# Sliding-window attention with a SwiGLU layer on one core: blocks 12 and 13 transposed by DMA, block 10 transposed three parts earlier, and another cut of the last output tile

## The chip, the cores and the metric

The kernel runs on one core of one Trainium2 chip. The metric is the device time of the kernel in microseconds (us). Before the change the median of three runs is 249.16 us (249.16 to 249.19). The profiled execution of the same kernel spans 248.5 us from its first to its last instruction, at a granted TensorE clock of 1.000.

## What is computed

Two stages, one behind the other. First attention with a sliding window of 128 keys and four "sink" keys that every query sees, for 4 batches, 8 heads, 768 positions and a head size of 64. Its output, laid out as 3072 tokens of 512 values, goes through an RMS norm and a gated layer:

```python
scores = scale * np.matmul(q, k.transpose(0, 1, 3, 2))
keep = is_sink | in_window          # in_window: 0 <= query - key < 128
a = softmax(np.where(keep, scores, -1e9));  x = a @ v
xn = x / np.sqrt(np.mean(x * x, axis=-1, keepdims=True) + 1e-06) * rms_g
g = xn @ w_gate
out = (g / (1 + exp(-g)) * (xn @ w_val)) @ w_out    # 512 -> 1536 -> 512
```

## The kernel before

**Blocks and groups.** The 3072 tokens are 24 blocks of 128 (`g` = 0 to 23; six to a batch, `b, t = divmod(g, 6)`). Four blocks make a group of 512 tokens (`G` = 0 to 5), which is what the gated layer works on. For a block, GpSimd issues the loads of q, k and v (`unit_load`; they become bf16 on the way), q and k are transposed so that the head dimension lies on the partitions (`unit_t`, into the tile `qkT` of the batch), TensorE makes the scores (`unit_s`, tile `pT`), ScalarE their exponentials (`et`), and TensorE multiplies by v (`unit_attend`, tile `pv`). VectorE divides by the sums (`rden`, `x`), ScalarE sums the squares (`sq`), VectorE makes the RMS scale and the scaled block (`xr`), and the block is transposed once more into `xnt` of its group (`unit_x`).

**Parts.** The gated layer of a group is a list of parts. A pair of parts for each slice of the hidden dimension is `gate` (tile `pg`, then tanh on ScalarE into `th`) and `val` (tile `pvl`, then two VectorE operations that give `p` and `hT`). They are followed by three parts for each output tile of 128 tokens (`parts_o`): 12 matmuls into `po`, a halving copy by ScalarE into `osb` (three buffers), and a store that SyncE issues. Group 0 comes as two halves of 256 tokens, `fa` and `fb`; the list of `fb` with the output tiles has 24 parts, 0 to 23. The later groups have 24 parts of `gate` and `val` and then 12 of output.

**Order.** `run(parts, slots)` walks the list of parts and ahead of part `s` calls the units whose slot number is `s` or lower, in the order of their numbers, and what is left after the last part. So attention for later blocks is woven by hand into the gated layer of an earlier group. For `fb` the slots are written out in `FIRST`; for later groups `step(g, p)` makes them, with `AT` giving each block its part. In group 1 the blocks 9 to 13 start at parts 0, 8, 14, 20 and 28. In these lists TensorE, SyncE and GpSimd keep the order as written (`MANUAL`), while the order of VectorE and ScalarE is set by the framework's planner, which takes an instruction when it reckons that its inputs are ready and takes the one written first when several are. In `fa` VectorE keeps the written order too.

**Transposes of q and k.** There are two ways. On TensorE: eight 128 x 128 transposes (L245) into one PSUM bank `pqk`, and a ScalarE copy of 128 x 1024 out of it (L279). By DMA: SyncE issues two transposing DMAs (L271), for q and for k, and TensorE and ScalarE do nothing. `by_dma(g)` says which; before, blocks from 14 on that don't start a batch go by DMA. `step` gives a TensorE transpose to the step two blocks earlier and a DMA transpose to the step three blocks earlier, four parts into it: block 12 comes at part 12 of group 1 and block 13 at part 18. Block 10 stands in `FIRST` at 21. Blocks 12, 13 and so on write `qkT` of their batch; two such tiles exist, and batch 2 takes the one that batch 0 had.

**PSUM.** One pool of eight banks serves all of TensorE's outputs; a matmul can wait for a bank that ScalarE or VectorE has yet to empty.

**The last tile.** `parts_last` cuts the last output tile into two halves of 256 columns. The first is copied by ScalarE and stored by SyncE. The second is copied in two pieces of 128 columns, by ScalarE (L698) and VectorE (L693), out of the same bank, and stored by two DMAs, from ScalarE's queue and from SyncE's.

**Semaphores of the DMAs.** The framework gives the DMAs of SyncE and ScalarE eight semaphores ("lanes") in turn, in the order in which they are issued. A DMA that takes a lane waits until the lane's previous DMA has landed. When the program ends (L904), SyncE waits for the lanes one after another, from the first to the eighth.

Of the kernel before, what the change touches and what calls it, by code (L numbers as in the profile page):

```python
# [9 lines left out]
ALU = mybir.AluOpType  # L10
ACT = mybir.ActivationFunctionType
FP32 = mybir.dt.float32
# [3 lines left out]
P = 128  # L16
# [12 lines left out]
def kernel(  # L29
# [13 lines left out]
    nc = tc.nc  # L43

    B, H, S, D = q.shape
    DM = H * D
# [4 lines left out]
    NT = S // P  # L51
    NB = B * NT
    HP = H // 2
    KTN = DM // P
    FTN = DFF // P
# [7 lines left out]
    NEG = -32768.0  # L63
    RMS_EPS = 1e-6 * RSQRT_SCALE ** 2
    MS_SCALE = RSQRT_SCALE / math.sqrt(DM)
    DMA_T_FROM = 14
    DMA_X_FROM = 12
    LD = 15
    FA = FTN
# [15 lines left out]
    opool = ctx.enter_context(tc.tile_pool(name="opool", bufs=3))  # L85
# [8 lines left out]
    wo = const.tile([P, FTN, DM], BF16, name="wo")  # L94
# [98 lines left out]
    with tc.manual_schedule(engines={mybir.EngineType.Pool, mybir.EngineType.DVE}):  # L193
        load_q(1)
        nc.gpsimd.affine_select(
            out=ident, in_=ident, compare_op=ALU.not_equal, fill=1.0,
# [3 lines left out]
            out=amasks[:, 1, 0, :], in_=amasks[:, 1, 0, :], compare_op=ALU.is_ge,  # L200
# [3 lines left out]
            out=amasks[:, 1, 1, :], in0=amasks[:, 1, 0, :], scalar1=-1.0, scalar2=NEG,  # L204
            op0=ALU.mult, op1=ALU.add,
# [17 lines left out]
            out=sel[:, P:P + NS], in_=sel[:, P:P + NS], compare_op=ALU.not_equal,  # L223
# [19 lines left out]
    def transposes(ps, src, c0):  # L243
        for hp in range(HP):
            nc.tensor.transpose(  # L245
                out=ps[:, c0 + hp * P:c0 + (hp + 1) * P],
                in_=src[:, 2 * hp:2 * hp + 2, :], identity=ident,
            )
# [11 lines left out]
        )  # L260

    def by_dma(g):
        return g >= DMA_T_FROM and g % NT > 0

    def unit_t(g):
        b, t = divmod(g, NT)
        if t == 0:
            QKT[b] = qkt.tile([P, 2, HP, S], BF16, name="qkT")
        if by_dma(g):
            for i, src in enumerate((QS.pop(g), KS_.pop(g))):  # L270
                nc.sync.dma_start_transpose(  # L271
                    out=QKT[b][:, i, :, t * P:(t + 1) * P],
                    in_=src.rearrange("p h d -> p (h d)"),
                )
            return
        ps = psum.tile([P, 512], FP32, name="pqk", tag="b1").bitcast(BF16)
        transposes(ps, QS.pop(g), 0)
        transposes(ps, KS_.pop(g), HP * P)
        nc.scalar.copy(  # L279
            out=QKT[b].rearrange("p i h s -> p (i h) s")[:, :, t * P:(t + 1) * P],  # L280
            in_=ps.rearrange("p (x c) -> p x c", c=P),
        )

    def unit_sink(b):
        ks = sink.tile([P, HP * KSW], BF16, name="ksk")
        nc.vector.memset(ks, 0.0)
        ksv = ks.rearrange("p (h c) -> p h c", c=KSW)
        for hi in range(2):
            pr = slice(hi * D, (hi + 1) * D)
            nc.scalar.copy(  # L290
                out=ksv[pr, :, hi * NS:(hi + 1) * NS],
                in_=QKT[b][pr, 1, :, 0:NS],
            )
        KSK[b] = ks
        vs = sink.tile([P, H, VW], BF16, name="vsk")
        for half in range(2):
            ps = psum.tile([P, 512], FP32, name="pvs", tag="b1")
            hs = slice(half * 4, half * 4 + 4)
            for i in range(4):
                h = half * 4 + i  # L300
                at = P - (32 * (h // 2) + NS * (h % 2))
                nc.tensor.matmul(
                    out=ps[:, i * VW:(i + 1) * VW], lhsT=sel[:, at:at + P],
                    rhs=V16[b][:, 0, h, :], start=True, stop=True,
                    skip_group_check=True,
                )
            nc.scalar.copy(
                out=vs[:, hs, :], in_=ps[:, 0:HW].rearrange("p (h c) -> p h c", c=VW),
            )
        VSK[b] = vs  # L310

    def unit_sink_scores(b, t):

        w = 2 * P
        ps = psum.tile([P, 512], FP32, name="pss", tag="b1")
        for hp in range(HP):
            nc.tensor.matmul(
                out=ps[32 * hp:32 * hp + KSW, 0:w],
                lhsT=KSK[b][:, hp * KSW:(hp + 1) * KSW],
                rhs=QKT[b][:, 0, hp, t * P:(t + 2) * P],  # L320
                start=True, stop=True,
            )
# [165 lines left out]
    def unit_attend(g):  # L488

        if g % NT >= 2:  # L490
            unit_sink_av(g)
        for u in range(2):
            unit_av(g, u)
# [139 lines left out]
    HT = {}  # L633
# [43 lines left out]

    def parts_last(G, tb):

        def half(c):  # L680
            po = psum.tile([P, 512], FP32, name="po", tag="b1")
            n = DM // 2
            for ft in range(FTN):
                nc.tensor.matmul(  # L684
                    out=po[:, 0:n], lhsT=HT[(G, ft // 2)][:, ft % 2, tb * P:(tb + 1) * P],
                    rhs=wo[:, ft, c * n:(c + 1) * n], start=(ft == 0), stop=(ft == FTN - 1),
                )
            row = (G * GB + tb) * P
            for i in range(1 + c):
                m = n // (1 + c)  # L690
                osb = opool.tile([P, m], FP32, name=f"ol{c}{i}", bufs=1)
                if i:
                    nc.vector.tensor_scalar(  # L693
                        out=osb, in0=po[:, i * m:(i + 1) * m], scalar1=0.5, scalar2=None,
                        op0=ALU.mult,
                    )
                else:
                    nc.scalar.mul(osb, po[:, 0:m], 0.5)  # L698
                (nc.sync, nc.scalar)[c - i].dma_start(
                    out=out[row:row + P, c * n + i * m:c * n + (i + 1) * m], in_=osb,  # L700
                )

        return [lambda: half(0), lambda: half(1)]

    def parts_o(G, tb):
        st = {}

        def part(i):
            if i == 0:
                st["po"] = psum.tile([P, 512], FP32, name="po", tag="b1")  # L710
            for ft in range(4 * i, 4 * i + 4):
                nc.tensor.matmul(  # L712
                    out=st["po"], lhsT=HT[(G, ft // 2)][:, ft % 2, tb * P:(tb + 1) * P],
                    rhs=wo[:, ft, :], start=(ft == 0), stop=(ft == FTN - 1),
                )
            if 4 * i + 4 == FTN:
                osb = opool.tile([P, DM], FP32, name="osb")

                nc.scalar.mul(osb, st["po"], 0.5)  # L719
                row = (G * GB + tb) * P  # L720
                nc.sync.dma_start(out=out[row:row + P, :], in_=osb)

        return [lambda i=i: part(i) for i in range(FTN // 4)]


    def step(g, p):

        b, t = divmod(g, NT)
        slots = [[] for _ in range(7)]
        if g < NB:  # L730
            if t in (2, 4):
                slots[0].append(lambda: unit_sink_scores(b, t))
            slots[0].append(lambda: unit_s(g))
            if t == 1:
                slots[2].append(lambda: unit_sink(b))
        if g <= NB:
            slots[0].append(lambda: unit_attend(g - 1))
        if g + 2 < NB and not by_dma(g + 2):
            slots[4].append(lambda: unit_t(g + 2))
        if g + 3 < NB and by_dma(g + 3):  # L740
            slots[4].append(lambda: unit_t(g + 3))
        for n in LOADS.pop(0) if LOADS else ():
            slots[1].append(lambda n=n: unit_load(n))
        return [(p + i, u) for i, us in enumerate(slots) for u in us]
# [14 lines left out]
    with tc.manual_schedule(engines=MANUAL_ALL):  # L759
# [35 lines left out]
            out=masks, in0=amasks, scalar1=-1.0 / NEG, scalar2=1.0,  # L795
            op0=ALU.mult, op1=ALU.add,
# [23 lines left out]
        (19, lambda: unit_x(5)),  # L820
        (19, lambda: unit_t(9)),
        (20, lambda: unit_attend(7)),
        (21, lambda: unit_t(10)),
        (22, lambda: unit_sink_scores(1, 2)),
        (22, lambda: unit_s(8)),
        (23, lambda: unit_x(6)),
# [27 lines left out]
    with tc.manual_schedule(engines=MANUAL):  # L854
# [54 lines left out]
```

The softmax here doesn't subtract the row's maximum and nothing guards it: scores larger than these inputs give would overflow.

## Time and profile before

| What | Value |
|---|---|
| Time, median of 3 | 249.16 us |
| Span of the profiled execution | 248.5 us |
| TensorE busy | 241.8 us, 97% |
| VectorE busy | 163.6 us, 66% |
| ScalarE busy | 145.2 us, 58% |
| GpSimd busy | 105.1 us, 42% |
| Group 1 (`pg` of group 1 to `pg` of group 2) | about 68.2 to 107.9 us: TensorE 39.70 of 39.70, ScalarE 28.43, VectorE 27.04 |
| ScalarE copies out of `pqk`, 128 x 1024 (L279) | 9, mean about 1.01 us |
| Transposing DMAs for q and k (L271) | 9 and 9, 1.22 us each on SyncE's queue (median), landing after 4.5 and 4.1 us (median), 2.4 at least and 8.8 at most |
| Stores of `osb`, 256 KB | 23, landing after 2.5 us (median) |

Times in views of the trace are us from the start of the span. Matmuls overlap in the records, since each one's end is modelled: what counts is from start to start. A name with q behind the engine (SPq, ACTq) is the engine's sequencer, which waits and issues DMAs. In square brackets stand the idle time of the engine before a row and what ended it.

### The profile page before, as it was taken

How to read it: one execution, taken by the hardware profiler on the slowest of the kernel's cores; microseconds unless marked ns; L12 is line 12 of the kernel's file. 1: busy time of each engine (PE TensorE's matmuls, PEld its weight loads, DVE VectorE, ACT ScalarE, POOL GpSimd, SP SyncE). 2: the span in 40 equal slices, each digit the busy share in tenths (PEclk: the TensorE clock that was granted, in tenths of full speed). 3: DMA queues.
4: the chain of work that ended last, by engine and by line, in shares of the span. 5: the costliest groups of instructions: out<-in, count | busy, mean ns of one | idle time of the engine just before them, and what ended most of it. 6: DMA issues, size and time to landing. Idle time of an engine off the chain costs nothing.

```text
span 248.5 us, 4926 instructions
## 1 busy us (share of the span) xinstructions
PE 241.8 (97%) x1850; PEld 129.5 (52%) x1850; DVE 163.6 (66%) x368; ACT 145.2 (58%) x336; POOL 105.1 (42%) x141
## 2 busy tenths in 40 slices
PE   7999999999999999999999999999999999999994
PEld 2566887856445554544454454444444444444443
DVE  5465896878467789339778368769167885387700
ACT  2779657898977774874674375674475242333221
POOL 8977676496398995970331000233231000000000
PEclk9999999999999999999999999999999999999999
DMA  9999999999959999599000694001610003500022
GB/s 128 153 171 192 190 160 187 183 155 188 126 69 144 148 129 161 91 161 164 0 3 12 158 168 88 0 4 22 190 46 0 3 0 63 190 3 0 0 86 84
DMA packets 102873, 24.96 MB, mean 100 GB/s; under 512 B 91841, under 2 KB 99905, under 8 KB 102850
## 3 DMA queue, kind: packets, MB, share of 16 engines
q0 software_dynamic: 80704, 13.90, 73.4%
q1 hardware_dynamic: 20962, 10.43, 18.4%
q10 hardware_dynamic: 1184, 0.33, 0.6%
q8 instruction: 14, 0.23, 0.4%
q14 instruction: 9, 0.07, 0.1%
HBM read 28.31 MB, written 6.29 MB: 139 GB/s over the span
## 4 chain that ended last, share of the span: by engine, by line
PE 90%; ACT 4%; DVE 2%; DMA 2%; issue 0%; ACTq 0%
PE pg L642 25%; PE pvl L642 25%; PE po L712 22%; PE pT L411 4%; PE pv L467 3%; PE pqk L245 2%; PE pv L471 2%; DMA osb<-in_q_dram 2%; ACT et L420 2%; PE pw L332 1%; PE po L684 1%; PE pT L342 1%; PE pv L453 1%; ACT sq L519 1%; PE pT L357 1%; PE pxt L612 1%
## 5 line engine op out<-in xcount | busy, mean ns | idle before, releaser
L642 PE MATMUL pg<-xnt,wg 128*128 128x512 bf16 (+1 forms) x336 | 74.2, 348 | 0.2 <-ACT xnt L630 0.2
L642 PE MATMUL pvl<-xnt,wv 128*128 128x512 bf16 (+1 forms) x336 | 74.0, 349 | 0.0
L660 DVE SCALAR_TENSOR_TENSOR p<-th,pg 128x512 bf16<-128x512 bf16 x72 | 49.3, 684 | 28.4 <-ACT th L655 28.0
L655 ACT ACTIVATE th<-pg 128x512 bf16<-128x512 f32 x72 | 43.3, 604 | 41.8 <-PE pg L642 40.6
L712 PE MATMUL po<-wo,hT 128*128 128x512 bf16 x276 | 63.2, 379 | 0.0
L670 DVE TENSOR_TENSOR hT<-p,pvl 128x512 bf16<-128x512 bf16 x72 | 49.5, 687 | 7.8 <-PE pvl L642 1.1
L388 POOL TENSOR_SCALAR_AFFINE_SELECT et<-et 128x512 bf16<-128x512 bf16 x28 | 19.0, 684 | 73.3 <-ACT et L420 73.3
L642 PEld LDWEIGHTS <-wv 128*128 128x128 bf16 x336 | 32.4, 98 | 29.6 <-issue 0.2
L642 PEld LDWEIGHTS <-wg 128*128 128x128 bf16 x336 | 31.4, 98 | 26.1 <-issue 1.0
L420 ACT ACTIVATE et<-pT 128x512 bf16<-128x512 f32 x76 | 39.5, 610 | 3.7 <-PE pT L411 3.6
L712 PEld LDWEIGHTS <-hT 128*128 128x128 bf16 x276 | 26.1, 98 | 28.8 <-issue 0.2
L719 ACT ACTIVATE osb<-po 128x512 f32<-128x512 f32 x23 | 13.8, 599 | 30.9 <-PE po L712 27.4
L519 ACT ACTIVATE sq<-x 128x256 bf16<-128x256 bf16 x48 | 20.4, 429 | 8.9 <-DVE x L508 8.5
L121 POOL DMA_DIRECT2D v<-in_v_dram x24 | 21.9, 913 | 3.8 <-DMA wo<-in_moe_w_out_dram 2.0
L108 POOL DMA_DIRECT2D qs<-in_q_dram x23 | 21.0, 911 | 4.7 <-DMA wo<-in_moe_w_out_dram 3.0
L108 POOL DMA_DIRECT2D ks<-in_k_dram x23 | 20.9, 907 | 1.9 <-issue 0.7
L503 DVE RECIPROCAL rden<-pv 128x4 f32<-128x4 f32 x48 | 7.5, 172 | 21.5 <-PE pv L471 21.3
L508 DVE TENSOR_TENSOR x<-pv,rden 128x256 bf16<-128x256 f32 x48 | 19.8, 422 | 1.0
L582 DVE SCALAR_TENSOR_TENSOR xr<-x,y,gb 128x512 bf16<-128x512 bf16 x22 | 16.9, 816 | 0.3
L393 POOL TENSOR_SCALAR_AFFINE_SELECT et<-et 128x512 bf16<-128x512 bf16 x22 | 14.8, 673 | 0.0
L471 PE MATMUL pv<-v,et 128*128 128x65 bf16 x168 | 12.6, 194 | 0.1
L411 PE MATMUL pT<-qkT 64*128 64x256 bf16 (+1 forms) x168 | 12.3, 262 | 0.2 <-ACT et L420 0.2
(83 smaller groups left out, 198.8 us busy)
## 6 DMA issues: line engine op xcount, KB each, us to landing
out_dram<-osb SPq DMA_DIRECT2D x23, 256.0 KB, 2.5
v<-in_v_dram POOLq DMA_DIRECT2D x24, 128.0 KB, 6.8
qs<-in_q_dram POOLq DMA_DIRECT2D x23, 128.0 KB, 6.4
ks<-in_k_dram POOLq DMA_DIRECT2D x23, 128.0 KB, 6.7
wg<-in_moe_w_gate_dram POOLq DMA_DIRECT2D x6, 256.0 KB, 8.1
wv<-in_moe_w_val_dram POOLq DMA_DIRECT2D x6, 256.0 KB, 8.4
wo<-in_moe_w_out_dram POOLq DMA_DIRECT2D x2, 768.0 KB, 10.4
osb<-in_k_dram ACTq DMA_DIRECT2D x1, 256.0 KB, 4.9
```

The costliest lines, as they stand in the source:

```text
L108: nc.gpsimd.dma_start(out=tl, in_=src[b, :, t * P:(t + 1) * P, :].rearrange("h t d -> t h d"),)
L121: nc.gpsimd.dma_start(out=V16[b][:, t, :, 0:D], in_=v[b, :, t * P:(t + 1) * P, :].rearrange("h t d -> t h d"),)
L388: nc.gpsimd.affine_select(out=ev[:, :, 0, :], in_=ev[:, :, 0, :], compare_op=ALU.is_ge, fill=0.0, base=0, pattern=[[0, x], [1, P]], channe ...
L411: nc.tensor.matmul(out=banks[u][hi][:, j * w:(j + 1) * w], lhsT=QKT[b][pr, 1, hp, t * P:(t + 1) * P], rhs=QKT[b][pr, 0, hp, t * P:t * P + ...
L420: nc.scalar.activation(out=et[:, hi].rearrange("p j n c -> p (j n c)"), in_=banks[u][hi], func=ACT.Exp, scale=inv_sqrt_d,)
L508: nc.vector.tensor_tensor(out=X16[g][:, heads_of(g, u), :], in0=pvv[:, :, 0:D], in1=RDEN.pop((g, u)).unsqueeze(2).to_broadcast((P, 4, D)), ...
L519: nc.scalar.activation(out=sq, in_=xh, func=ACT.Square, scale=MS_SCALE, accum_out=MS[g - i][:, i, u:u + 1],)
L642: nc.tensor.matmul(out=ps[:, i * n:(i + 1) * n], lhsT=w_sb[:, kt, ft * P:(ft + 1) * P], rhs=XNT[G][:, kt, cols], start=(kt == 0), stop=(kt ...
L655: nc.scalar.activation(out=st["th"], in_=st["pg"], func=ACT.Tanh, scale=0.5)
L660: nc.vector.scalar_tensor_tensor(out=p1, in0=st["th"], scalar=1.0, in1=st["pg"], op0=ALU.add, op1=ALU.mult,)
L670: LAST[0] = nc.vector.tensor_tensor(out=HT[key][:, i:i + n, cols], in0=p1.rearrange("p (n c) -> p n c", n=n), in1=pvl.rearrange("p (n c) - ...
L712: nc.tensor.matmul(out=st["po"], lhsT=HT[(G, ft // 2)][:, ft % 2, tb * P:(tb + 1) * P], rhs=wo[:, ft, :], start=(ft == 0), stop=(ft == FTN ...
```

## The change

Five edits. Blocks 12 and 13 are transposed by DMA rather than on TensorE, and their transposes are written behind the last part of group 0. Block 10 stays on TensorE and goes from part 21 to part 18 of `FIRST`. The last tile is cut into 384 and 128 columns, both copied by ScalarE, the first stored by SyncE and the second from ScalarE's queue. The stores of the first two tiles of group 4 are each cut into two of 64 rows. `step` leaves out the blocks that now stand in `FIRST`. The purpose is to take transposes off TensorE, to spread ScalarE's copies where the first group ends, to shorten what follows the last matmul, and to have the last DMA on the last lane, which is what the two additional stores are for.

```diff
-    DMA_T_FROM = 14
+    DMA_T_FROM = 12
@@
     def by_dma(g):
-        return g >= DMA_T_FROM and g % NT > 0
+        return g >= DMA_T_FROM and g != 3 * NT
@@ parts_last
-        def half(c):
+        def cols(c):
             po = psum.tile([P, 512], FP32, name="po", tag="b1")
-            n = DM // 2
+            lo, hi = ((0, 3 * P), (3 * P, DM))[c]
             for ft in range(FTN):
                 nc.tensor.matmul(
-                    out=po[:, 0:n], lhsT=HT[(G, ft // 2)][:, ft % 2, tb * P:(tb + 1) * P],
-                    rhs=wo[:, ft, c * n:(c + 1) * n], start=(ft == 0), stop=(ft == FTN - 1),
+                    out=po[:, 0:hi - lo], lhsT=HT[(G, ft // 2)][:, ft % 2, tb * P:(tb + 1) * P],
+                    rhs=wo[:, ft, lo:hi], start=(ft == 0), stop=(ft == FTN - 1),
                 )
             row = (G * GB + tb) * P
-            for i in range(1 + c):
-                m = n // (1 + c)
-                osb = opool.tile([P, m], FP32, name=f"ol{c}{i}", bufs=1)
-                if i:
-                    nc.vector.tensor_scalar(
...
-                else:
-                    nc.scalar.mul(osb, po[:, 0:m], 0.5)
-                (nc.sync, nc.scalar)[c - i].dma_start(
-                    out=out[row:row + P, c * n + i * m:c * n + (i + 1) * m], in_=osb,
-                )
+            osb = opool.tile([P, hi - lo], FP32, name=f"ol{c}", bufs=1)
+            nc.scalar.mul(osb, po[:, 0:hi - lo], 0.5)
+            (nc.sync, nc.scalar)[c].dma_start(out=out[row:row + P, lo:hi], in_=osb)
@@ parts_o
-                nc.sync.dma_start(out=out[row:row + P, :], in_=osb)
+                n = P // 2 if G == 4 and tb < 2 else P
+                for r in range(0, P, n):
+                    nc.sync.dma_start(out=out[row + r:row + r + n, :], in_=osb[r:r + n])
@@ step
-        if g + 2 < NB and not by_dma(g + 2):
-            slots[4].append(lambda: unit_t(g + 2))
-        if g + 3 < NB and by_dma(g + 3):
-            slots[4].append(lambda: unit_t(g + 3))
+        for n in (g + 2, g + 3):
+            if n < NB and n not in (10, 12, 13) and by_dma(n) == (n == g + 3):
+                slots[4].append(lambda n=n: unit_t(n))
@@ FIRST
-        (21, lambda: unit_t(10)),
+        (18, lambda: unit_t(10)),
+        (24, lambda: unit_t(12)),
+        (24, lambda: unit_t(13)),
```

More of the change, by code (lines that the diff above doesn't have):

```diff
@@ L678, in parts_last @@
     def parts_last(G, tb):
-        def half(c):
+        def cols(c):
             po = psum.tile([P, 512], FP32, name="po", tag="b1")
-            n = DM // 2
+            lo, hi = ((0, 3 * P), (3 * P, DM))[c]
             for ft in range(FTN):
                 nc.tensor.matmul(
-                    out=po[:, 0:n], lhsT=HT[(G, ft // 2)][:, ft % 2, tb * P:(tb + 1) * P],
-                    rhs=wo[:, ft, c * n:(c + 1) * n], start=(ft == 0), stop=(ft == FTN - 1),
+                    out=po[:, 0:hi - lo], lhsT=HT[(G, ft // 2)][:, ft % 2, tb * P:(tb + 1) * P],
+                    rhs=wo[:, ft, lo:hi], start=(ft == 0), stop=(ft == FTN - 1),
                 )
             row = (G * GB + tb) * P
-            for i in range(1 + c):
-                m = n // (1 + c)
-                osb = opool.tile([P, m], FP32, name=f"ol{c}{i}", bufs=1)
-                if i:
-                    nc.vector.tensor_scalar(
-                        out=osb, in0=po[:, i * m:(i + 1) * m], scalar1=0.5, scalar2=None,
-                        op0=ALU.mult,
-                    )
-                else:
-                    nc.scalar.mul(osb, po[:, 0:m], 0.5)
-                (nc.sync, nc.scalar)[c - i].dma_start(
-                    out=out[row:row + P, c * n + i * m:c * n + (i + 1) * m], in_=osb,
-                )
-        return [lambda: half(0), lambda: half(1)]
+            osb = opool.tile([P, hi - lo], FP32, name=f"ol{c}", bufs=1)
+            nc.scalar.mul(osb, po[:, 0:hi - lo], 0.5)
+            (nc.sync, nc.scalar)[c].dma_start(out=out[row:row + P, lo:hi], in_=osb)
+        return [lambda: cols(0), lambda: cols(1)]
     def parts_o(G, tb):
```

## The prediction

> **What bounds the kernel now.** I read the shares of busy time and the chain first, then the timeline of TensorE around the moved transposes, then TensorE and ScalarE where the first group ends, then the SyncE queue and the last microseconds. The page:
>
> ```profile
> PE 241.8 (97%) x1850; PEld 129.5 (52%) x1850; DVE 163.6 (66%) x368; ACT 145.2 (58%) x336; POOL 105.1 (42%) x141
> ...
> PE 90%; ACT 4%; DVE 2%; DMA 2%; issue 0%; ACTq 0%
> ```
>
> TensorE carries the chain nearly everywhere, so work taken off it shortens the kernel, unless another engine then stops it. Its busy share can hide short waits, so I look at starts. The timeline of TensorE where block 12 is transposed (start, duration):
>
> ```profile
> 79.57 1.03 PE L642 MATMUL pvl<-xnt,wv 128*128 128x512 bf16 x4
> 80.43 0.39 PE L245 MATMUL pqk<-ident,qs 128*128 128x128 bf16 x4
> 80.66 0.39 PE L245 MATMUL pqk<-ident,ks 128*128 128x128 bf16 x4
> 80.88 1.03 PE L642 MATMUL pg<-xnt,wg 128*128 128x512 bf16 x4
> ```
>
> No gap: eight transposes push the next matmul from 80.43 to 80.88, 0.45 us, or 56 ns each. The rows for block 13 (87.09 to 87.54) say the same. The one place where TensorE waits after its first group starts is the group's end:
>
> ```profile
> 65.75 0.54 PE L411 MATMUL pT<-qkT 64*128 64x256 bf16 x5
> 66.50 0.38 PE L411 MATMUL pT<-qkT 64*128 64x256 bf16 x3 [0.22 <-ACT et L420]
> 66.99 0.27 PE L453 MATMUL pv<-vsk,esk 64*128 64x260 bf16 x1
> 67.47 0.27 PE L453 MATMUL pv<-vsk,esk 64*128 64x260 bf16 x1 [0.21 <-ACT xnt L621]
> ...
> 68.16 0.38 PE L642 MATMUL pg<-xnt,wg 128*128 128x512 bf16 x1
> ```
>
> From the first pT to the next pg are 2.41 us; the same sequence at block 10 (75.83 to 76.98) takes 1.15. So 1.26 us are waits for ScalarE to empty PSUM. ScalarE there:
>
> ```profile
> 58.87 0.61 ACT L621 COPY xnt<-pxt 128x512 bf16<-128x512 bf16 x1
> 59.35 0.45 ACT L519 ACTIVATE sq<-x 128x256 bf16<-128x256 bf16 x1
> ...
> 60.24 1.05 ACT L279 COPY qkT<-pqk 128x1024 bf16<-128x1024 bf16 x1
> 62.42 0.42 ACT L519 ACTIVATE sq<-x 128x256 bf16<-128x256 bf16 x1 [1.14 <-DVE x L508]
> ...
> 63.71 1.00 ACT L279 COPY qkT<-pqk 128x1024 bf16<-128x1024 bf16 x1
> ...
> 64.88 2.06 ACT L420 ACTIVATE et<-pT 128x512 bf16<-128x512 f32 x4
> 66.78 0.63 ACT L621 COPY xnt<-pxt 128x512 bf16<-128x512 bf16 x1
> ```
>
> It idles 1.14 us before 62.42, then works without a pause, and the copy at 63.71 is block 10's: it stands before the et and xnt that TensorE waits for. SyncE, which issues the transposing DMAs:
>
> ```profile
> 54.08 14.20 SPq L721 DMA_DIRECT2D out_dram<-osb  x4
> 74.74 2.37 SPq L271 DMA_TRANSPOSE qkT<-qs  x1
> ```
>
> Its queue is empty from 68.28 to 74.74. The end of the kernel:
>
> ```profile
> 243.88 1.86 SPq L699 DMA_DIRECT2D out_dram<-ol  x2
> 244.79 0.28 ACT L698 ACTIVATE ol<-po 128x128 f32<-128x128 f32 x1 [0.93 <-PE po L684]
> 245.09 0.36 ACTq L699 DMA_DIRECT2D out_dram<-ol  x1
> 245.10 0.29 DVE L693 TENSOR_SCALAR ol<-po 128x128 f32<-128x128 f32 x1 [9.46 <-ACT ol L698]
> ```
>
> The two evictions of the last half don't overlap: VectorE starts when ScalarE ends, and the last store is issued at 245.41.
>
> **What the Trainium skill says.** "PSUM — Partial Sum Buffer", PSUM bank collisions: two engines must not touch one bank and quadrant at once, readers included, so software orders them. The trace agrees: VectorE starts 0.03 us after ScalarE ends. "Perfetto Trace Analysis", Per-engine timelines (HWDGE): the recorded window of a DMA instruction covers descriptor generation, not data movement. The trace agrees: a transpose holds SyncE 1.2 us and lands after 2.4 to 8.8 (median 4.5 and 4.1). "TensorE: Matmul & The Clock Gate", Back-to-back issue gap, puts a stream of 128-column matmuls with weight loads at about 81 ns each; this trace shows 56 for the transposes, each with its own load, and I use 56.
>
> **The change, part by part.**
>
> *Blocks 12 and 13 by DMA.* TensorE loses 16 transposes: 16 x 56 ns = 0.90 us, at two places without a gap. ScalarE loses two copies of 1.01; they aren't on the chain there. VectorE is dense from 90 to 96 (hT of part 11 ends at 95.99, its first reader starts at 96.34), but its work is released by TensorE and ScalarE and moves up with them. SyncE gains four transposes behind the first group's last store, which is issued at 67.94. The loads of blocks 12 and 13 land by 62.15 and 65.52, so nothing is waited for: four of 1.2 to 2.4 us end at 73 to 78. Behind them stand block 14's, which wait for their own load until 74.74 anyway and are first used after 106. Block 12's scores read both blocks at 89.36 (about 87.5 then). Even the slowest case, 68.3 + 4 x 2.37 + 8.8 = 86.6, is in time; the likely one, 73 + 4.5 = 77.5, by far. Cost zero; gain 0.90.
>
> *Block 10 at part 18 instead of 21.* The same eight transposes, so TensorE neither gains nor loses by itself. Its q and k land at 55.88 and 56.74; the transposes come at about 57.54, so they don't wait. What moves is ScalarE's copy, which holds the engine from 63.71 to 64.60, 0.89 us. ScalarE's order is the planner's. After xnt at 58.87 it took sq (59.35) though the next xnt's transposes were done at 58.7: the older work goes first when it is ready. I take it that block 10's copy then comes behind that sq, and with xnt and block 9's copy fills the idle 1.14 us (59.8 + 0.47 + 0.89 + 1.05 = 62.2, before 62.42). Everything from 63.71 on is then 0.89 earlier, TensorE's last wait ends at 66.58 instead of 67.47. Block 9's copy ends at 62.2 and its first reader starts at 62.70. Gain 0.89 likely; bounds 0 (copy ahead of sq, which pushes the idle along with it) and 1.26.
>
> *Last tile in 384 + 128 columns.* Matmuls: 24 of 256 columns took 2.63 us, 110 ns each; 12 x 162 (between 110 and 216, estimated by columns) + 12 x 56 = 2.62, the same. The 384-column eviction (0.49, between 0.38 for 256 and 0.60 for 512) starts at about 244.1 and ends before the last one starts at 244.79. Gone is the VectorE eviction, 0.29 + 0.03. The last store is then the ScalarE one, issued at 245.09, landing 1.6 later at 246.70; before, SyncE saw the last landing at 247.035. Gain 0.33. The 384-column store, issued at 244.6, should land about 1.85 later (1.70 for 128 KB, 2.0 for 256 KB), at 246.45, but shares the DMA engines with the last one: up to 0.15 lost.
>
> *Last lane last.* DMAs from SyncE and ScalarE take eight semaphores in turn; at the end SyncE waits for them in order. Before there are 59 DMAs and the last has the third: after its landing at 247.035 five more checks follow, 0.06 apart, to 247.338. With 4 transposes and 2 half stores more and one store less there are 64, so the last has the eighth and nothing follows. Gain 0.30. The two half stores of group 4 cost SyncE 2 x 0.4 us; ScalarE's fourth osb of that group waits for the first store (214.12), perhaps 0.3 longer, and th behind it at 214.69 too. TensorE waits for that th only through the PSUM banks, and in group 5 a th comes every 1.73 us and takes 0.6: hidden, cost zero.
>
> Sum: 0.90 + 0.89 + 0.33 + 0.30 - 0.10 = 2.32 us; 249.16 - 2.32 = 246.84.
>
> **Rivals.** (1) *The copy of block 10 goes ahead of sq.* Then sq, block 6's norm, block 7's norm and the idle time all move by about 0.9, and et and xnt come when they came. Gain 0.90 + 0.53: 247.73. For it: sq was ready only 0.05 before it started. Against it: ScalarE chose sq then. (2) *The boundary waits grow.* The moved copy delays xr of block 7 (it ends at 65.21; TensorE needs it at 65.43), costing up to 0.7; et of block 8 slips by another copy, 0.89; and the later th of group 5 isn't hidden, 0.45. Then 249.16 - 1.43 + 2.04 = 249.77, slower. Against it: it needs a new order of ScalarE at two places. (3) *Something takes up what TensorE gives.* In the second group another engine bounds (VectorE from 90 to 96) and block 10's move brings nothing: only the tail's 0.53 stays, 248.63. Against it: the 28 us that VectorE waited for th on the page.
>
> **How the numbers follow.** Forecast 0.62, rival 1 0.23, rival 3 0.07, rival 2 0.08. The likeliest gives 246.84. Low end: 1.26 instead of 0.89 at the boundary, nothing lost in the tail: 246.37, so 246.4. High end: rival 1 with 0.3 less in the tail, 248.0. Faster by over 0.2% means under 248.66: forecast, rival 1 and half of rival 3, 0.88; rival 3's other half and some of rival 2, 0.05; slower 0.07.
>
> **What would show it.** Two groups of L245 in the second group gone and its span 0.9 shorter; four transposes on SyncE before 78; pT to pg at the boundary near 1.5 us with the L279 copies together before 62.4; no VectorE row at the end and no check after the last store's landing. A wait of L411 for qkT at block 12, or a pause of TensorE at 57.5 or after 213, would make it wrong.

## The result, and the profile after

| | before | after |
|---|---|---|
| Time, median | 249.47 us (249.16 to 250.09, 6 runs) | 247.29 us (247.00 to 247.74, 6 runs) |
| Span of the profiled execution | 248.5 us | 245.4 us |
| Span start to first `pg` | 17.57 us | 16.42 us |
| Group 0, first `pg` to first `pg` of group 1 | 50.59 us | 50.26 us |
| Group 1, to first `pg` of group 2 | 39.58 us | 38.85 us |
| The rest, to the end | 140.72 us | 139.92 us |

The ratio is 0.9911, 95% interval 0.9893 to 0.9929: 2.2 us gained, at a forecast of 2.32. The two spans differ by 3.0 us, because the profiled execution of the kernel before was a late one (250.16 us, a span of 248.5; the executions of it that ran beside the experiments span 247.1 to 248.8, most of them under 248.2). What differs is the head, whose code the change doesn't touch: in the traces of all kernels here the first `pg` comes 16.3 to 17.6 us after the start. So below I count from the first `pg`. From there to the end it is 230.89 us before and 229.03 after: **1.86 us** come from the change. (By the medians it is 2.2 us here and 1.7 when the kernel is run again below.)

The page of the kernel after, shares of busy time and the chain:

```profile
PE 239.0 (97%) x1809; PEld 127.8 (52%) x1834; DVE 163.2 (66%) x367; ACT 143.8 (59%) x334; POOL 105.3 (43%) x141
...
PE 87%; DVE 5%; issue 3%; ACT 3%; POOL 1%; ACTq 0%; POOLq 0%
```

TensorE still carries the chain, but VectorE's share has gone from 2% to 5%: it has become the one that TensorE waits for, in places. The timeline of TensorE in group 1 where block 12's transposes stood:

```profile
78.26 1.03 PE L642 MATMUL pvl<-xnt,wv 128*128 128x512 bf16 x4
79.13 1.03 PE L642 MATMUL pg<-xnt,wg 128*128 128x512 bf16 x4
79.99 1.03 PE L642 MATMUL pvl<-xnt,wv 128*128 128x512 bf16 x4
```

`pg` follows `pvl` after 0.87 us and nothing lies between. SyncE's queue (start, duration) has the four transposes right behind the first group's stores, without a pause:

```profile
53.02 13.39 SPq L713 DMA_DIRECT2D out_dram<-osb  x4
66.53 1.30 SPq L271 DMA_TRANSPOSE qkT<-qs  x1
67.93 1.20 SPq L271 DMA_TRANSPOSE qkT<-ks  x1
69.23 1.22 SPq L271 DMA_TRANSPOSE qkT<-qs  x1
70.54 1.22 SPq L271 DMA_TRANSPOSE qkT<-ks  x1
74.25 1.19 SPq L271 DMA_TRANSPOSE qkT<-qs  x1
```

The end of group 0 on TensorE:

```profile
65.16 0.61 PE L411 MATMUL pT<-qkT 64*128 64x256 bf16 x8
65.61 0.27 PE L453 MATMUL pv<-vsk,esk 64*128 64x260 bf16 x2
...
66.45 0.20 PE L471 MATMUL pv<-v,et 128*128 128x65 bf16 x1 [0.19 <-POOL et L388]
...
66.68 0.81 PE L642 MATMUL pg<-xnt,wg 128*128 128x512 bf16 x3
```

From the first `pT` to the next `pg` it is 1.52 us rather than 2.41. The three waits for ScalarE are gone. What is left, 0.37 us more than the 1.15 of the undisturbed sequence, is a wait for a mask of GpSimd. ScalarE there:

```profile
58.43 0.42 ACT L519 ACTIVATE sq<-x 128x256 bf16<-128x256 bf16 x1
...
58.85 0.99 ACT L279 COPY qkT<-pqk 128x1024 bf16<-128x1024 bf16 x1
59.74 0.59 ACT L621 COPY xnt<-pxt 128x512 bf16<-128x512 bf16 x1
60.22 1.02 ACT L279 COPY qkT<-pqk 128x1024 bf16<-128x1024 bf16 x1
61.47 0.42 ACT L519 ACTIVATE sq<-x 128x256 bf16<-128x256 bf16 x1 [0.23 <-DVE rden L503]
...
61.88 0.58 ACT L709 ACTIVATE osb<-po 128x512 f32<-128x512 f32 x1
62.36 0.40 ACT L519 ACTIVATE sq<-x 128x256 bf16<-128x256 bf16 x1
```

Both copies out of `pqk` stand ahead of the former idle time, which has shrunk from 1.14 to 0.23 us. The end of the kernel on ScalarE:

```profile
241.91 0.49 ACT L690 ACTIVATE ol<-po 128x384 f32<-128x384 f32 x1 [1.35 <-PE po L684]
242.58 0.28 ACT L690 ACTIVATE ol<-po 128x128 f32<-128x128 f32 x1 [0.18 <-PE po L684]
242.89 0.36 ACTq L691 DMA_DIRECT2D out_dram<-ol  x1
```

The last eviction waits for TensorE alone. The 384-column store is issued at 242.43 and lands at 244.30, the last one is issued at 242.89 and lands at 244.52, and the kernel ends 0.93 us later (1.42 before, from SyncE's sight of the last landing).

### The profile page after: what moved, and what is told of

Read it like the earlier page. It is cut to its first block, busy times and chain, and to the rows that moved or that the text cites. A ratio compares the mean times of both kernels' runs of the same rounds, so it can differ in the third digit from the quotient of the medians.

```text
span 245.4 us, 4880 instructions
## 1 busy us (share of the span) xinstructions
PE 239.0 (97%) x1809; PEld 127.8 (52%) x1834; DVE 163.2 (66%) x367; ACT 143.8 (59%) x334; POOL 105.3 (43%) x141
## 4 chain that ended last, share of the span: by engine, by line
PE 87%; DVE 5%; issue 3%; ACT 3%; POOL 1%; ACTq 0%; POOLq 0%
PE pg L642 24%; PE pvl L642 24%; PE po L702 22%; PE pT L411 4%; PE pv L467 2%; PE pv L471 2%; PE pw L332 2%; PE pqk L245 2%; PE po L684 1%; ACT sq L519 1%; DVE hT L670 1%; PE pv L453 1%; ACT et L420 1%; PE pT L357 1%; DVE x L508 1%
## 5 line engine op out<-in xcount | busy, mean ns | idle before, releaser
L702 PE MATMUL po<-wo,hT 128*128 128x512 bf16 x267 | 62.2, 379 | 0.4
```

The source lines that it names most:

```text
L702: nc.tensor.matmul(out=st["po"], lhsT=HT[(G, ft // 2)][:, ft % 2, tb * P:(tb + 1) * P], rhs=wo[:, ft, :], start=(ft == 0), stop=(ft == FTN ...
```

## The reader that the prediction had overlooked

Everything that was named had happened, and yet the two stages gave 1.06 us rather than 1.79. Group 1 is 0.73 shorter, not 0.90. ScalarE at the start of group 1 in the kernel after:

```profile
68.18 0.69 ACT L655 ACTIVATE th<-pg 128x512 bf16<-128x512 f32 x1
...
70.38 0.41 ACT L290 COPY ksk<-qkT 64x16 bf16<-64x16 bf16 x2 [1.11 <-DMA qkT<-ks]
70.82 0.60 ACT L655 ACTIVATE th<-pg 128x512 bf16<-128x512 f32 x1
```

Two tiny copies (64 x 16, 0.41 us together) take the sink keys of a batch out of `qkT` (`unit_sink`). For batch 2 they read block 12's k. They are written at part 30 of group 1, but ScalarE's order is the planner's, and there they stand ahead of the second tanh of the group. So ScalarE waits 1.11 us for the transposing DMA, and the tanh behind it is late. VectorE waits for that tanh, then runs without a pause up to the next step of attention:

```profile
69.70 0.69 DVE L670 TENSOR_TENSOR hT<-p,pvl 128x512 bf16<-128x512 bf16 x1
71.45 0.69 DVE L660 SCALAR_TENSOR_TENSOR p<-th,pg 128x512 bf16<-128x512 bf16 x1 [1.06 <-ACT th L655]
...
74.25 0.68 DVE L660 SCALAR_TENSOR_TENSOR p<-th,pg 128x512 bf16<-128x512 bf16 x1
```

When TensorE comes to the second `pv` of that step, VectorE still reads the bank (until 74.93). The two `pv` of a step can start together (they do in the run no_1213 below, at 74.56 both); here the first starts at 74.80 and the second at 74.98, 0.18 later. The trace of the kernel before had the reader in plain sight, on ScalarE, right behind the copy that is removed:

```profile
81.08 1.01 ACT L279 COPY qkT<-pqk 128x1024 bf16<-128x1024 bf16 x1 [0.65 <-PE pqk L245]
82.00 0.60 ACT L655 ACTIVATE th<-pg 128x512 bf16<-128x512 f32 x1
82.50 0.40 ACT L290 COPY ksk<-qkT 64x16 bf16<-64x16 bf16 x2
```

## The experiments

All kernels below are the kernel after with the edit shown. Stages in us, from the starts on TensorE's timeline; time is the median against its own runs of before.

| Kernel | time | ratio (95%) | group 0 | group 1 | rest | first `pg` to end |
|---|---|---|---|---|---|---|
| before | 249.47 | | 50.59 | 39.58 | 140.72 | 230.89 |
| after | 247.29 | 0.9911 (0.9893 to 0.9929) | 50.26 | 38.85 | 139.92 | 229.03 |
| after_again | 247.61 | 0.9931 (0.9916 to 0.9945) | 50.40 | 38.87 | 139.90 | 229.17 |
| no_1213 | 247.68 | 0.994 (0.9925 to 0.9955) | 50.17 | 39.57 | 139.93 | 229.67 |
| t10_at_21 | 248.36 | 0.9956 (0.9941 to 0.9971) | 50.78 | 39.25 | 139.91 | 229.94 |
| old_tail | 248.03 | 0.9945 (0.993 to 0.996) | 50.23 | 38.86 | 140.37 | 229.46 |
| lane_first | 247.85 | 0.9939 (0.9923 to 0.9955) | 50.09 | 38.86 | 140.35 | 229.30 |
| t10_at_20 | 247.20 | 0.992 (0.9903 to 0.9936) | 49.91 | 39.25 | 139.89 | 229.05 |
| mask_order | 247.64 | 0.9929 (0.9915 to 0.9944) | 50.03 | 39.25 | 139.92 | 229.20 |
| t11_dma | 254.12 | 1.0191 (1.017 to 1.0213) | 50.07 | 45.67 | 139.90 | 235.64 |
| sink_late | 247.52 | 0.9926 (0.9906 to 0.9946) | 50.39 | 38.68 | 139.90 | 228.97 |
| t11_sink_late | 248.01 | 0.9928 (0.9897 to 0.9958) | 50.23 | 40.08 | 139.92 | 230.23 |
| t11_t20_late | 246.36 | 0.988 (0.9856 to 0.9903) | 49.87 | 38.24 | 139.89 | 228.00 |
| t11_t20_late_again | 246.59 | 0.9875 (0.9858 to 0.9891) | 49.77 | 38.24 | 139.93 | 227.94 |

The stages behind group 0 repeat far better than the times: groups 2 to 4 agree within 0.02 us in all traces, while the medians of one and the same kernel differ by 0.3. There the stages decide where a few tenths matter. Group 0 varies more: in the eight traces here with block 10 at part 18 and the masks in their old order it takes 50.07 to 50.40 us, though the code of the stage differs at most in its last lines. With block 10 at part 21 it is 50.59 and 50.78.

### The same kernel once more: after_again

No edit.

> The changed kernel as it is, as the control for the kernels of this call. Theory: the gain over the kernel before is the sum of four parts that don't touch each other (0.9 us from the transposes of blocks 12 and 13, 0.4 to 0.9 from block 10's copy, 0.3 from the cut of the last tile, 0.3 from the last lane), so about 2.0 to 2.4 us below the kernel before on the same chip. Rival: over 0.5 us of the first measured difference came from a start that varies from execution to execution; then it is 1.5 us or less here. In the trace, wherever the first group's TensorE work starts before about 16.5 us, TensorE waits for the load of block 10's k at its transposes (0.46 us were seen); where it starts a microsecond later, it doesn't.

Group 1 and the rest come again within 0.02 us; group 0 is 0.14 longer. It waits at another place. After shows, on TensorE at block 10's transposes:

```profile
56.49 0.39 PE L245 MATMUL pqk<-ident,qs 128*128 128x128 bf16 x4
57.18 0.40 PE L245 MATMUL pqk<-ident,ks 128*128 128x128 bf16 x4 [0.30 <-DMA ks<-in_k_dram]
```

By the starts TensorE lost 0.46 us to the load of block 10's k (eight transposes take 0.45 from start to start when nothing is missing; here the second half began 0.69 after the first instead of 0.22). In after_again that pause is absent, and its timeline has another in its place:

```profile
63.77 1.03 PE L702 MATMUL po<-wo,hT 128*128 128x512 bf16 x3
65.29 0.40 PE L612 MATMUL pxt<-ident,xr 128*128 128x128 bf16 x4 [0.49 <-DVE xr L582]
```

From `po` to the next `pxt` are 1.52 us; in after the same two are at 63.98 and 64.84, 0.86 apart. TensorE gets to block 7's transposes before VectorE has `xr` ready, and loses 0.65 us by the starts. VectorE is late since ScalarE puts an `osb` (61.88 in the listing above) between the two `sq` of block 7, which were back to back before. Either way 0.5 to 0.65 us of the boundary's 0.89 are spent elsewhere in the same stage. Which of the two waits comes depends on the head: the loads don't move with the first `pg`. Block 10's k lands at 56.74 to 57.56 us after the start in all fourteen traces, whether the first `pg` comes at 16.27 or at 17.57. In the traces with block 10 at part 18 where the first `pg` comes at 16.27 to 16.56 us, the transposes of k are held up by 0.2 to 0.5 us; at 16.68 it is 0.1, and from 16.79 on it is 0.06 or nothing. The wait of `ksk`, 1.1 us, is there again.

### Only block 10 moved: no_1213

```diff
-    DMA_T_FROM = 12
+    DMA_T_FROM = 14
-            if n < NB and n not in (10, 12, 13) and by_dma(n) == (n == g + 3):
+            if n < NB and n != 10 and by_dma(n) == (n == g + 3):
-        (24, lambda: unit_t(12)),
-        (24, lambda: unit_t(13)),
-                n = P // 2 if G == 4 and tb < 2 else P
+                n = P // 2 if G == 4 or G == 3 and tb < 2 else P
```

> Blocks 12 and 13 are transposed on TensorE again, at their old parts of the second group; all else is as in the changed kernel, with six half stores instead of two so that the last DMA still has the last lane. Theory: the 16 transposes come back at 56 ns each with nothing beside them: the second group is 0.7 to 0.9 us longer and the time 0.7 to 0.9 us longer than the changed kernel's. Rival (another engine takes up what TensorE gives): no change beyond 0.3 us.

Group 1 returns to 39.57 us, the value before: its whole gain is that of blocks 12 and 13. Block 10's move alone has given 0.42 us in group 0, again after waits for loads (0.30 for q and 0.49 for k, by the starts on TensorE).

### Only block 10 put back: t10_at_21

```diff
-        (18, lambda: unit_t(10)),
+        (21, lambda: unit_t(10)),
```

> Only block 10's transposes go back to part 21. Theory: ScalarE's copy of block 10 stands again before the et of block 8, so that the wait of TensorE where the first group ends grows from about 0.37 to 1.26 us, while the wait for block 10's load goes away: 0.4 us slower than the changed kernel where that wait was 0.46, 0.9 slower where there was none. Rival (the move only trades one wait for another): the same time within 0.2 us.

The waits of the boundary are back (2.57 us from the first `pT` to the next `pg`) and group 0 is 0.52 longer than in after. But group 1 is longer as well, 39.25, although it has no transposes of blocks 12 and 13: the second `pv` starts 0.57 us behind the first rather than 0.18. (The expectation of t11_t20_late puts this wait at 0.46; the 0.46 in the expectation above is another one, that for block 10's k.) So with blocks 12 and 13 by DMA, group 1 gets 0.73 or only 0.33 of the 0.90.

### The last tile: old_tail and lane_first

old_tail has the two halves of before at the end, and one pair of half stores rather than two, so that the last DMA is on the last lane all the same:

```diff
-        def cols(c):   # 384 + 128 columns, two evictions by ScalarE
+        def half(c):   # 256 + 256, the second evicted by ScalarE and VectorE
...
-                n = P // 2 if G == 4 and tb < 2 else P
+                n = P // 2 if G == 4 and tb < 1 else P
```

> The last tile is cut as before (256 columns, then two evictions of 128 by ScalarE and VectorE), with one half-store pair instead of two, so that there are 64 DMAs and the last one still has the last lane. Theory: from the start of ScalarE's last eviction to the last landing 2.25 us instead of 1.96, so 0.3 us slower; nothing after the landing. Rival (the gain at the end is the lane's alone): no change.

The rest is 0.45 longer than after: 0.30 from the last matmul's start to the last landing (2.50 against 2.20), and 0.19 from there to the end (1.12 against 0.93), less 0.04 elsewhere. The 0.19 goes with VectorE's `drain`, an instruction that stands at the end of every engine's work in these traces. In old_tail and in before, where VectorE makes the last eviction, its `drain` is the last of all, from 0.35 to 0.22 us before the end; in the twelve other traces it is done 0.47 to 0.49 us before the end, and GpSimd's is the last. The rest is also 0.35 shorter than before, which differs from it in the lanes. So the cut is worth 0.45 and the lanes 0.35. lane_first checks the lanes from the other side, with one more store ahead of the last, so that this one gets the first lane and seven checks follow:

```diff
-                n = P // 2 if G == 4 and tb < 2 else P
+                n = P // 2 if G == 4 and tb < 3 else P
```

> The changed kernel with one store of group 4 more cut in two: 65 DMAs, so the last one has the first lane instead of the eighth. Theory: seven checks of SyncE follow the last landing, 0.06 us apart, so that from the last landing to SyncE's drain there are about 0.5 us instead of 0.08, and from the last landing to the end 1.35 instead of 0.9; 0.43 us slower. Rival (the lanes don't matter, the end barrier waits for something else): the same end.

Last landing to end is 1.36 us (244.39 to 245.75) against 0.93: 0.43 more, 0.061 per check.

### What else holds group 0: t10_at_20 and mask_order

```diff
-        (18, lambda: unit_t(10)),
+        (20, lambda: unit_t(10)),
```

> Block 10's transposes at part 20 instead of 18. Theory: the part of the boundary's gain that came back did so because the transposes stand at the landing of block 10's k, and because ScalarE then puts an eviction between the two sq of block 7, which makes xr of block 7 late. At part 20 the load has landed 3 us before, and the copy still fits into ScalarE's idle time: no wait for ks, none for xr, so from the first pg to the second group's first pg 49.7 to 49.9 us instead of 50.3 to 50.4, and 0.4 to 0.6 us faster than the changed kernel. Rival (what came back is due to the start of the execution or to GpSimd's masks alone): 50.2 to 50.4, no gain.

Two parts later there is neither a wait for the load nor for `xr`, and ScalarE runs the two `sq` of block 7 together. One wait of TensorE for ScalarE's `xnt` is back at the boundary, 0.48 us by the starts, but group 0 falls to 49.91 us. mask_order has GpSimd do the masks that are needed first before the others of the block:

```diff
         if nq == 2:
-            nc.gpsimd.affine_select(
-                out=ev[:, :, 1, :], in_=ev[:, :, 1, :], ...
+            late.append(lambda: nc.gpsimd.affine_select(   # called behind the loop over u
+                out=ev[:, :, 1, :], in_=ev[:, :, 1, :], ...
```

> The changed kernel with GpSimd's masks in another order: for each block first the two that its own attention needs, then the two for the next block. Theory: the wait of pv at the end of the first group (0.37 us, for the third of block 8's masks) goes, and the first group is 0.35 us shorter than the changed kernel's (50.26 and 50.40 us from first pg to next group's pg): about 49.95. Rival (TensorE then waits for something else there, the bank or xr): no gain.

The wait for the mask is gone (from the first `pT` to the next `pg` it is 1.18 us); one of 0.24 for `xr` remains; group 0 is 50.03, only just below the 50.07 to 50.40 of the eight traces. Both kernels got shorter in group 0 and lost it in group 1, which rose to 39.25, with 0.57 at the second `pv`. Counted from the first `pg`, that `pv` starts at 58.56 us in after, 58.60 in t10_at_20 and 58.73 in mask_order, whenever TensorE arrives at the step. That it waits for VectorE's `p` is in each trace that shows the wait, as here in t10_at_20:

```profile
75.07 0.27 PE L453 MATMUL pv<-vsk,esk 64*128 64x260 bf16 x1 [0.30 <-DVE p L660]
```

The second `pv` keeps step with SyncE instead: in all seven traces where block 12 is the first to go by DMA and the planner places the sink copies, it starts 8.45 to 8.47 us after the first of the four transposing DMAs, and that one 1.14 to 1.15 us after ScalarE starts the last `osb` of group 0. From there the way goes over the landing of block 12's k, the sink copies, the tanh behind them and VectorE's row of `p` and `hT`. The last `osb` came no earlier in the two kernels (49.01 and 49.12 us after the first `pg`, against 48.97 in after). While the sink copies wait for their DMA, what TensorE alone gains at the boundary is lost again at that point.

### One more block by DMA: t11_dma

```diff
-        return g >= DMA_T_FROM and g != 3 * NT
+        return g >= DMA_T_FROM - 1 and g != 3 * NT
-            if n < NB and n not in (10, 12, 13) and by_dma(n) == (n == g + 3):
+            if n < NB and n not in (10, 11, 12, 13) and by_dma(n) == (n == g + 3):
+        (24, lambda: unit_t(11)),
         (24, lambda: unit_t(12)),
-                n = P // 2 if G == 4 and tb < 2 else P
+                n = P
```

> Block 11 goes by DMA too, ahead of 12 and 13; its two DMAs take the place of the two half stores, so there are still 64. Theory (TensorE sets the pace of the second group): eight transposes less, the group is 0.45 us shorter, 38.4 instead of 38.86, and so is the time. Rival (the six transposes on SyncE land too late for block 10's scores, which read block 11's q 7 us after the first is issued): the scores wait and the group isn't shorter.

The gain didn't come: 254.12 us, with all the loss in group 1. The list of waits from 64 to 115 us:

```profile
ACT ksk L290 <- DMA qkT<-ks: 6.0, 1, 6.0
...
PE pT L411 <- DVE p L660: 3.5, 1, 3.5
```

Block 11's two DMAs stand ahead of block 12's on SyncE's queue, so that block 12's k is issued 2.6 us later; it also takes longer, 5.5 us from its issue to the sink copies rather than 2.45. These wait 5.98 us instead of 1.11, the tanh behind them are late by as much, VectorE waits 5.34 us for one of them, and TensorE stops for 3.61 us (by its starts) for want of a bank. Then it goes on at half its clock:

```profile
80.50 1.90 PE L642 MATMUL pg<-xnt,wg 128*128 128x512 bf16 x4
...
83.89 1.43 PE L642 MATMUL pg<-xnt,wg 128*128 128x512 bf16 x4
85.15 1.03 PE L642 MATMUL pvl<-xnt,wv 128*128 128x512 bf16 x4
```

From 80.90 to 84.3 a matmul of 512 columns takes 426 or 427 ns from start to start rather than 216; the granted clock is 0.50 from 77.86 to 84.69 and 1.00 before and behind that. The pause and the half clock (TensorE is busy for 6.11 us of it, so some 3.1 are lost) account for nearly all of the 6.8 us against after.

### The cause taken away: sink_late, t11_sink_late, t11_t20_late

The waits named above are a chain in one trace; these three kernels test it. The sink copies of batch 2 are held behind the tanh last written, which is far from the DMA and still 12 us ahead of their reader:

```diff
+        with tc.issue_after(TH[0]) if b == 2 else nullcontext():
             for hi in range(2):
                 pr = slice(hi * D, (hi + 1) * D)
                 nc.scalar.copy(
@@ gate
-            nc.scalar.activation(out=st["th"], in_=st["pg"], func=ACT.Tanh, scale=0.5)
+            TH[0] = nc.scalar.activation(
+                out=st["th"], in_=st["pg"], func=ACT.Tanh, scale=0.5,
+            ).ins
```

> The kernel after, with one edit: ScalarE's two copies into ksk of batch 2 (the sink keys, read out of block 12's transposed k) may not be issued before the tanh of part 22 of group 1. Theory S: in the kernel after these copies stand at 70.38 us, in front of two tanh, and wait 1.11 us for the transposing DMA of block 12's k; the tanh behind them come late, VectorE's p comes late, and TensorE waits 0.17 us for the bank at block 10's second pv. Then the wait is gone, pg to pg of group 1 falls from 38.86 to 38.67 to 38.72 us (before less 0.9), and first pg to end from 229.0 to 229.2 falls to 228.85 to 229.0. Rival V: VectorE itself is full there, the wait stays and group 1 stays at 38.86. Time: S about 247.2, V about 247.4, too close to tell by the time alone; the stage tells.

Group 1 is 38.68 us, 0.90 below before, to the hundredth what the removed transposes cost. ScalarE goes from one tanh to the next:

```profile
68.77 0.69 ACT L659 ACTIVATE th<-pg 128x512 bf16<-128x512 f32 x1
...
70.05 0.60 ACT L659 ACTIVATE th<-pg 128x512 bf16<-128x512 f32 x1 [0.19 <-PE pg L646]
```

Rival V is out. The time, 247.52, doesn't show it: in this trace group 0 has the wait for `xr` (0.63), and 0.17 is below what four runs resolve.

> The kernel that had block 11 transposed by DMA as well (254.1 us), with the sink copies held back as in sink_late. Theory S: the whole 5 us came from ScalarE standing 5.98 us at the sink copies, behind which the tanh of group 1 waited; without it group 1 is another eight transposes shorter than in sink_late, 38.68 - 0.45 = 38.2 us, first pg to end about 228.4, time about 246.7. Rival: the scores of block 10, which read block 11, or the banks wait for the six transposing DMAs; then TensorE still pauses in front of 77.9 us, group 1 stays above 42 us, and the time near 253.

With block 11 by DMA as well, the pause in front of 77.9 us and the half clock are gone. So the sink copies were the cause of the whole loss, not the scores and not the queue. But the number was missed: group 1 is 40.08 rather than 38.2, and the runs spread from 246.2 to 249.1 us. In the trace another wait of TensorE has come in, 1.84 us (by its starts) in front of a `pxt` at 100.52. The profile puts its end to VectorE's `x` at 100.04, so what was missing is likely the bank that `x` reads. That `x` stands behind an `xr` that took long. VectorE's four `xr` in that stretch are in the second line (in ns: shortest, median, longest):

```profile
100.52 0.40 PE L615 MATMUL pxt<-ident,xr 128*128 128x128 bf16 x4 [1.68 <-DVE x L511]
...
L585 DVE SCALAR_TENSOR_TENSOR xr<-x,y,gb x4: 746/749/3208, 94.7 to 96.7; 128x512 bf16<-128x512 bf16 x4
```

The last takes 3.21 us, from 96.70 to 99.91, and GpSimd's timeline has a load's issue and four masks in that time:

```profile
96.08 0.88 POOL L121 DMA_DIRECT2D v<-in_v_dram  x1
96.96 0.65 POOL L391 TENSOR_SCALAR_AFFINE_SELECT et<-et 128x512 bf16<-128x512 bf16 x1
97.55 0.65 POOL L396 TENSOR_SCALAR_AFFINE_SELECT et<-et 128x512 bf16<-128x512 bf16 x1
98.14 0.64 POOL L391 TENSOR_SCALAR_AFFINE_SELECT et<-et 128x512 bf16<-128x512 bf16 x1
98.72 0.63 POOL L396 TENSOR_SCALAR_AFFINE_SELECT et<-et 128x512 bf16<-128x512 bf16 x1
```

It ends 0.56 us after the last of them. That this is what spreads the times is likely but argued from one trace.

> As t11_sink_late, and block 10 transposed at part 20 rather than 18. With block 10 at 20 the first group took 49.91 us rather than 50.26 in the kernel after, but the time hardly fell, since block 10's second pv then waited 0.46 rather than 0.17 us for a bank. Theory S: that wait, too, came from the tanh late behind the sink copies; with them out of the way both gains stay: group 0 49.9, group 1 38.2, first pg to end about 228.05, time about 246.3. Rival V: VectorE or a bank takes the 0.35 back in group 1 (38.5), time 246.7, no better than t11_sink_late.

Both gains stay: group 0 is 49.87 and group 1 is 38.24. What t10_at_20 gained in group 0 and lost again at the second `pv` stays gained. In this trace all four `xr` take 0.74 to 0.75 us and are done at 96.53; it is GpSimd's first mask, from 96.08, that takes 0.94 us instead of 0.63.

> The same kernel as t11_t20_late in more executions, since that one had four and t11_sink_late, which differs from it by the part of block 10 alone, spread from 246.2 to 249.1 us. If the gain is that of the stages (group 0 about 49.9 us, group 1 about 38.24, first pg to end about 228.0), the median is 246.2 to 246.6 and the stages come again. Rival: what lengthened t11_sink_late's profiled execution, one xr of VectorE that took 3.21 us rather than 0.75 or 1.12 while GpSimd ran four masks, belongs to block 11's transposes by DMA and hits this kernel too; then part of the executions lie 1.5 to 2.5 us higher, the median is above 247, and group 1 is near 40 in a trace that has such an xr.

The stages come again (49.77, 38.24, 227.94 in all), no `xr` of that stretch is long, and four runs lie between 246.23 and 246.69 us. The interval of its ratio, 0.9858 to 0.9891, lies just below that of after, 0.9893 to 0.9929: block 10 at part 20, block 11 by DMA and the sink copies held back make a kernel that beats before and after, the latter by 0.7 to 1.25 us by the medians and 1.0 to 1.2 by the stages. Eight executions don't exclude that the long `xr` hits it now and then.

## Why the prediction was right, and where it wasn't

The time, 247.29 for 246.84, lies in the range, and the case was the forecast, not a rival: block 10's copy went ahead of the idle time, behind the `sq`. The sum was 2.32 and the stages give 1.86. Term by term:

- **Blocks 12 and 13, 0.90.** Measured 0.73 in group 1, and 0.90 in sink_late: the price of the transposes was exact. The step that failed is "nothing is waited for". It named the scores as the first reader of block 12 and left out `ksk`, whose wait of 1.11 us costs TensorE 0.18. It cost little because this case happened to put block 12 first on the queue; t11_dma shows the same wait at 5.98 us and a loss of 6.8. So the slack of ten microseconds that the prediction computed (77.5 to 87.5) was none.
- **Block 10, 0.89.** At the boundary it is 0.89 (2.41 to 1.52), and the order on ScalarE is the one reasoned out. That it fits to the hundredth is luck: all 1.26 us of waits for ScalarE went, not 0.89 of them, since TensorE itself came there later, by its wait for block 10's k (in t10_at_20, without such a wait, 0.48 for ScalarE is left); and 0.37 for GpSimd's mask came in, which the prediction didn't have. Over group 0 it is 0.33 (0.19 in after_again; 0.68 to 0.82 in the three traces with block 10 at part 20). The step that failed is "the transposes come at about 57.54, so they don't wait": they came at 56.49, and the k they need landed in time for 57.18. Counted from the first `pg` they came when forecast (40.07 us; 57.54 is 39.97 behind the first `pg` of before), but the load is counted from the program's start, and the profile that the prediction read has the latest first `pg` of all traces here. Where they don't wait, rival 2's delay of `xr` comes in, 0.65 in after_again and 0.63 in sink_late. The prediction gave the full amount at one place to the whole stage.
- **The cut of the last tile, 0.33 less 0.10.** Measured 0.45. The landing gave 0.30 as forecast, the expected collision of the two last stores didn't show (1.87 us for 384 columns, for which 1.85 was estimated), and 0.19 came on top between landing and end. This goes with the late `drain` of VectorE, which the prediction didn't have; why it is late there stays open.
- **The last lane, 0.30.** Measured 0.35 and, from the other side, 0.43 for seven checks.
- **The half stores, nothing.** Right: from group 5's first `pg` to the last matmul's start it is 31.05 us against 31.00.

Of the signs that were named, all but two came as told. The pause of TensorE near 57.5, which was to make the prediction wrong, appeared at 56.7 and did take its share; and group 1 was shorter by 0.73 rather than 0.9. Rival 3 named VectorE between 90 and 96 us; it held TensorE up at 75 instead, and for another reason.

Block 10's shortfall (0.56) and the sinks' (0.17) are met in part by the tail's surplus (0.80 measured in the rest, 0.53 forecast); that the sum came near is luck.

## What to carry to other kernels

When a tile's producer moves to another queue, list every reader of that tile in the old trace, the tiny ones too, and look at what is queued behind each on its engine; the first reader by the new order counts, and a planner may move it when its input changes hands. A wait removed at one place is worth in full only if the next engine to arrive is as early: count the whole stage, start to start, and look for the next wait in it. Where the head of a program varies by a microsecond, compare stages, not spans, and expect loads that are issued early to be nearer or farther from their readers by as much.

## What the runs showed of the hardware that was not expected

- A pause of 3.61 us of TensorE in the middle of a dense kernel (t11_dma) was followed by 6.83 us at a granted clock of 0.50. The Trainium skill, "TensorE: Matmul & The Clock Gate", What's actually happening, says that the clock is halved after at least one idle window of about 3.4 us and is full again after at least one busy window of that length. The trace agrees with the first, at 426 to 427 ns for 512 columns against 216. The full clock came back after twice the 3.4 us, though TensorE was busy for 6.11 of the 6.83.
- `xr` of VectorE and the masks of GpSimd lengthen each other. `xr`, which reads two operands from SBUF, takes 0.75 us in most places, 1.12 at some in every trace, each time beside a mask, and once 3.21 beside four masks; a mask beside it takes up to 1.2 rather than 0.63. The Trainium skill, "SBUF — State Buffer", Who interferes with whom, says that a VectorE instruction with two SBUF inputs contends with a GpSimd instruction that reads SBUF. The trace agrees. In the one case of 3.21 us `xr` ended only behind the fourth mask in a row.
- Each lane check at the end of the program costs 0.06 us (0.43 for seven in lane_first). The time from start to first `pg`, with the same code, varied between 16.3 and 17.6 us.
